# The local heads' v in alternate partitions: two requests a unit, keys in token order, a tile of its own

## The chip, the core and the metric

The kernel runs on one NeuronCore of one Trainium2 chip. The metric is the device time of one execution in microseconds (us). Five engines work beside each other: TensorE (PE; its weight loads are listed apart as PEld), VectorE (DVE), ScalarE (ACT), GpSimd (POOL) and SyncE (SP). SP issues all the DMA requests here. The profile is one execution with the hardware profiler on.

## What is computed

Three stages in float32, the output of each being the input of the next:

- Attention: B=4, 8 heads, S=576 tokens, D=64. Heads 0 to 3 are local (a query sees itself and the 31 tokens before it), heads 4 to 7 are strided (a query sees the earlier tokens with the same position modulo 32).
- A soft mixture of experts on the 2304 x 512 result: 8 experts with 4 slots each.
- A relu-squared layer, 512 to 2048 to 512.

```python
mask_local = (rel >= 0) & (rel < 32)              # rel = query position - key position
mask_strided = (rel >= 0) & (pos_k % 32 == pos_q % 32)
attn = softmax(where(mask, q @ k.T / 8, -1e9));  x = attn @ v
logits = x @ phi                                  # 2304 x 32
slot_in = softmax(logits, over tokens).T @ x      # 32 slots
slot_out = relu(slot_in @ w1[e]) @ w2[e]          # e: expert of the slot
y = softmax(logits, over slots) @ slot_out
out = relu(y @ w_in) ** 2 @ w_out
```

## The kernel before

**Units.** Attention is cut into 16 units of two heads of one batch. Units with an even number are local, those with an odd number strided. Each unit goes through short stages, and a table of token lists interleaves the stages of neighbouring units. The stages that matter here, for a local unit: `Tk`/`Tq` transpose k and q on PE (L504, L506), `k`/`q` copy them out of PSUM into `kTl` and `qTl` (64 features of head 0 on partitions 0 to 63, of head 1 on 64 to 127, all in the tile `space`); `S` computes scores (`st_S`, L557); `s` takes the maximum and adds it (`st_s`, L600); `e` exponentiates; `PT` transposes the weights into `Tl`; `p` copies; `A` multiplies by v (`st_A`, L677).

**Scores.** A local unit has 18 blocks of 32 queries. Each block sees 64 keys (its own 32 and the 32 before) of both heads, 128 columns in all: the moving operand of L566 is `kTl[:, :, 32qb:32qb+64]`, 64 columns of head 0 and then 64 of head 1. Each matmul runs as two instructions, so a unit has 36, in four streams (`tile_position`). The mask is added by matmuls in front (L562, L563). Within a block of 32 the keys lie with the 16 even tokens first and then the 16 odd ones.

**v of local units.** `vL` is a part of `space` with 128 partitions, 18 blocks and two heads of 65 columns (64 of v, and a column of ones that gives the softmax sum). Head h has partitions 64h to 64h+63: the upper 32 of them hold the block's own keys, the lower 32 the keys of the block before. `load_v` (L399) reads the block's own keys with four requests a unit: for each head one for the even and one for the odd tokens, each with 16 neighbouring partitions x 18 blocks x 256 bytes (72 KB). `shift_v` (L410) then copies on POOL, for each head, 32 partitions x 17 blocks x 64 columns from the upper 32 partitions to the lower, one block later. `vL` is single: the next local unit's load comes after the `A` of the one before.

**Order.** A scheduler sets SP's order of requests, the compute engines keep an order that is written out. Every SP request takes one of eight DMA lanes and waits for the request eight before it; where it overwrites a buffer it also waits for the engines that read it.

**Weights.** The experts' weights (w1 and w2, 64 requests of 512 KB) are fetched through SP into 27 ring slots and, as attention buffers retire, into the 16 slots of 4 KB a partition (`NA`) that make up `space` (`fetch`, L266, `give`, L299). After attention the first expert layer (L1055) frees slots for the last weights, the second (L1085) ends when they are there, and the last stage (L1241, L1283) follows on PE until the end.

Of the kernel before, what the change touches and what calls it, by code (L numbers as in the profile page):

```python
# [19 lines left out]
RING = 27  # L20
NA = 16
SPARE = 0
# [15 lines left out]
def kernel(  # L38
# [29 lines left out]

    space = wexp.enter_context(tc.tile_pool(name="space", bufs=1)).tile([128, NA * 1024], F32, name="space")
    at = [1024 * SPARE]  # L70
# [77 lines left out]
    def fill_last(n):  # L148
        if not n or spare[0] is None:
            return  # L150
        ps, c0 = spare[0]
        for _ in range(n):
            nc.tensor.matmul(
                out=ps[:, 1, c0:512], lhsT=identb,
                rhs=maskl.rearrange("p t h w -> p (t h w)")[:, 0:512 - c0], start=True, stop=True,
            )
# [109 lines left out]
    def fetch(n=RING):  # L266
        while stream and n:
            key = stream[-1]
            is_w = key[0] in ("w1", "w2")
            ring_ok = n_live[0] < (RING if is_w or key in so_[0:2] else late_cap[0])  # L270
            if is_w and free and not (ring_ok and given[0] == NA):
                r = free.pop(0)
                t = space[:, ts(r, 1024)]
# [40 lines left out]
    identb = cp.tile([128, 128], BF16, name="identb")  # L314
    identp = cp.tile([128, 128], BF16, name="identp")
    delta = cp.tile([128, 32], F32, name="delta")
# [5 lines left out]
    phi4 = cp.tile([128, KD, 4, NS], F32, name="phi4")  # L322
    none = cp.tile([128, 32], BF16, name="none")
    lN = cp.tile([128, B, 5, 32], F32, name="lN")
# [27 lines left out]
    ends["S", NU - 1] = at[0]  # L352
    vL, Pl, Tl = part(128, 18, 2, 65), part(128, 5, 2, 64), part(128, S)
    ends["A", NU - 2] = at[0]
# [4 lines left out]
    ends["X", NU - 1] = at[0]  # L359
    maskl = cp.tile([128, 5, 2, 64], BF16, name="maskl")  # L360
    assert at[0] <= NA * 1024, at[0]

# [27 lines left out]
    def load_v(u):  # L390
        if u >= NU:
            return
        b, p = units[u]
        for h in range(2):
            src = v[b, 2 * p + h]
            if local(u):
                for e in range(2):
                    r = 64 * h + 32 + 16 * e
                    nc.sync.dma_start(  # L399
                        out=vL[r:r + 16, :, h, 0:D], in_=src.rearrange("(b i e) d -> e i b d", i=16, e=2)[e]  # L400
                    )
            else:
                nc.sync.dma_start(
                    out=vS[64 * h:64 * h + 36], in_=src.rearrange("(p c) d -> p c d", c=16)
                )

    def shift_v(u):
        if local(u):
            for h in range(2):
                (nc.vector if on("vs", u)[h] else nc.gpsimd).tensor_copy(  # L410
                    vL[64 * h:64 * h + 32, 1:18, h, 0:D], vL[64 * h + 32:64 * h + 64, 0:17, h, 0:D]
                )

    def conv_in():
# [13 lines left out]
        done(key)  # L428

    load(0)  # L430
    load(1)
# [14 lines left out]
    for h in range(2):  # L446
        nc.vector.memset(kTl[ts(h, 64), h, 0:32], 0.0)
        nc.vector.memset(vL[64 * h:64 * h + 32, 0, h, 0:D], 0.0)
        nc.vector.memset(vL[ts(h, 64), :, h, D:D + 1], 1.0)
    nc.vector.memset(none, 0.0)  # L450
# [8 lines left out]
    for g in range(4):  # L459
        w_ = mf[ts(g, 32)].rearrange("p (b e i) -> p b e i", b=2, e=2)  # L460
        diag(w_, [[32, 2], [1, 2], [2, 16]], 0, NEG, op=ALU.is_gt, cm=-1)
        diag(w_, [[-32, 2], [-1, 2], [-2, 16]], 32, NEG, op=ALU.is_ge, cm=1)
    nc.vector.tensor_copy(
        maskl.rearrange("p t h w -> p (t h) w"), tmp[:, None, 0:64].to_broadcast([128, 10, 64])
    )
    nc.vector.memset(maskl[0:32, 0, :, 0:32], NEG)
    for g in range(4):
# [46 lines left out]

    def halves_(t, ps):

        for h in range(2):
            for e in range(2):
                o = t[ts(h, 64), h] if len(t.shape) == 3 else t[ts(h, 64)]
                i = ps[ts(e, 64), h].rearrange("c (j x) -> c j x", j=2)[:, :, 0:144]  # L520
                yield (
                    2 * h + e, o.rearrange("c (n e p j) -> c e n p j", e=2, p=8, j=2)[:, e],
                    i.rearrange("c j (n p) -> c n p j", p=8),
                )
# [32 lines left out]
    def st_S(u):  # L557
        ps = hold("s", u)
        if local(u):
            pf = flat(ps)[:, 0:640]  # L560
            mk = maskl.rearrange("p t h w -> p (t h w)")
# [33 lines left out]
    def st_s(u):  # L595
        ps = held.pop(("s", u))
        mx = ap_.tile([128, 16], F32, tag="mx", name="mx", bufs=3)
        if local(u):
            pv = flat(ps)[:, 0:640].rearrange("p (n w) -> p n w", w=64)
            nc.vector.tensor_reduce(out=mx[:, 0:10], in_=pv, axis=AX.X, op=ALU.max, negate=True)  # L600
            nc.vector.tensor_tensor(
                out=Pl.rearrange("p t h w -> p (t h) w"), in0=pv,
                in1=mx[:, 0:10, None].to_broadcast([128, 10, 64]), op=ALU.add,
            )
            return
# [14 lines left out]
    def st_e(u):  # L620
        P = Pl.rearrange("p t h w -> p (t h) w") if local(u) else Pe
        nc.scalar.activation(out=P, in_=P, func=AF.Exp)
# [13 lines left out]
    def st_PT(u):  # L636
        ps = hold("p", u)
        pf = flat(ps)
        if local(u):
            for t in range(5):  # L640
                nc.tensor.transpose(  # L641
                    out=pf[:, ts(t, 128)], in_=Pl[:, t].rearrange("p h w -> p (h w)"), identity=ident
                )
# [290 lines left out]
    def emit(u, token):  # L934
# [38 lines left out]
        elif what in ("S", "A"):  # L973
            give(what, v)

    for token in ("Tk+1", "k+1", "Tq+1", "q+1"):
# [358 lines left out]
```

## Time and profile before

| | |
|---|---|
| median of 3 runs | 407.06 us (402.96, 407.34, 407.06) |
| the profiled execution | 406.62 us, of which 404.9 us are the span from first to last instruction |
| mean granted TensorE clock | 0.975 of full speed |
| PE busy | 382.0 us, 94% of the span |
| DVE, ACT, POOL busy | 243.5, 235.0, 106.3 us |
| DMA | 69.88 MB, mean 173 GB/s |
| v of local units (L399) | 32 requests of 72 KB |
| chain that ended last, by line | L1283 47%, expert weights 10%, L1241 4%, v 4%, L677 2% |

A busy share is an average over the whole span. The attention stage ends near 140 us, the expert weights near 172 us, and from there to the end PE works almost without a gap, so the views of the first 175 us are read apart.

### The profile page before, as it was taken

The numbers are of one execution on the slowest core, as the hardware profiler recorded it, in microseconds if no ns is written. First come the engines' busy times: TensorE is split into PE (matmuls) and PEld (weight loads), VectorE is DVE, ScalarE is ACT, GpSimd is POOL, SyncE is SP. The second block draws the span as 40 slices with busy tenths as digits, with TensorE's granted clock in tenths as the row PEclk, the third lists the DMA queues.
The fourth block names the chain that finished last, engine by engine and source line by source line (L and its number), as shares of the span: only waits on it lengthen the run. The fifth ranks groups of instructions, "written<-read, shape, count | busy, mean of one in ns | idle before, by whom it ended". The sixth has DMA issues, their size and how long they took to land.

```text
span 404.9 us, 9258 instructions
## 1 busy us (share of the span) xinstructions
PE 382.0 (94%) x3649; PEld 301.0 (74%) x3649; DVE 243.5 (60%) x458; ACT 235.0 (58%) x491; POOL 106.3 (26%) x174
## 2 busy tenths in 40 slices
PE   7899999998947999999999999999999999999996
PEld 5688878877736635477787888888788888788885
DVE  5447588778743441158865666775768666755534
ACT  3457667766330320068777777667666766667670
POOL 6710221022002020035504544007522055320000
PEclk9689999999985999999999999999999999999999
DMA  7898899998999999997213203111000000003124
GB/s 159 256 281 200 258 268 236 284 250 237 402 319 357 355 345 418 418 418 284 104 53 105 88 31 132 64 53 53 2 0 2 1 0 2 0 26 131 63 94 155
DMA packets 38891, 69.88 MB, mean 173 GB/s; under 512 B 13312, under 2 KB 23808, under 8 KB 38848
## 3 DMA queue, kind: packets, MB, share of 16 engines
q1 hardware_dynamic: 38848, 69.29, 52.8%
q8 instruction: 29, 0.48, 0.5%
q14 instruction: 14, 0.11, 0.1%
HBM read 64.55 MB, written 4.72 MB: 171 GB/s over the span
## 4 chain that ended last, share of the span: by engine, by line
PE 68%; DMA 17%; DVE 5%; ACT 3%; POOL 2%; SPq 2%; issue 2%; DVEq 0%; POOLq 0%; ACTq 0%
PE banks L1283 47%; DMA w<-in_moe_w_dram 10%; DMA space<-in_v_dram 4%; PE banks L1241 4%; PE banks L677 2%; PE banks L504 2%; ACT space L492 2%; DMA space<-in_k_dram 2%; PE banks L506 2%; DVE space L662 1%; POOL space L410 1%; SPq L388 1%; PE banks L722 1%; PE banks L641 1%; DVE part L1297 1%
## 5 line engine op out<-in xcount | busy, mean ns | idle before, releaser
L1283 PE MATMUL banks<-w 128*128 128x512 f32 x867 | 217.0, 393 | 1.1 <-POOL w L1133 0.6
L1283 PEld LDWEIGHTS banks<-w 128*128 128x128 f32 x867 | 159.8, 188 | 36.6 <-DVE w L1257 1.5
L1257 DVE TENSOR_TENSOR w<-r,w 128x384 fp32r<-128x384 f32 (+1 forms) x97 | 59.3, 618 | 54.7 <-ACT w L1256 54.5
L1248 ACT ACTIVATE r<-banks 128x384 f32<-128x384 f32 (+1 forms) x96 | 47.0, 490 | 53.9 <-PE banks L1241 45.3
L492 ACT COPY space<-banks 64x288 f32<-64x288 f32 (+2 forms) x80 | 37.0, 463 | 32.8 <-DVE space L492 10.8
L1254 ACT ACTIVATE r<-r 128x384 f32<-128x384 f32 (+1 forms) x96 | 50.3, 524 | 3.0
L1256 ACT CAST w<-r 128x384 fp32r<-128x384 f32 (+1 forms) x97 | 49.5, 511 | 3.8 <-DVE r L1253 0.3
L410 POOL COPY space<-space 32x1088 f32<-32x1088 f32 x16 | 17.6, 1097 | 90.8 <-DMA space<-in_v_dram 66.4
L1297 DVE TENSOR_TENSOR part<-banks,part 128x512 f32<-128x512 f32 (+1 forms) x55 | 35.1, 675 | 1.9 <-PE banks L1283 1.9
L1241 PE MATMUL banks<-cT,A 128*128 128x384 f32 x96 | 32.0, 335 | 0.0
L220 POOL TENSOR_SCALAR nm<-w 128x512 f32<-128x512 f32 x28 | 21.6, 773 | 27.3 <-DVE w L227 14.7
L223 DVE TENSOR_SCALAR nm<-nm 128x512 uint32<-128x512 uint32 x32 | 14.7, 458 | 21.7 <-POOL nm L220 21.7
L1132 POOL CAST w<-wf 128x512 fp32r<-128x512 f32 x16 | 12.9, 809 | 50.5 <-PE banks L1283 27.1
L504 PE MATMUL banks<-ident,space 128*128 128x128 f32 x128 | 22.6, 304 | 1.3 <-DMA space<-in_q_dram 1.3
L1133 POOL TENSOR_TENSOR w<-wf,w 128x512 fp32r<-128x512 f32 x16 | 23.1, 1442 | 1.4
L224 DVE SCALAR_TENSOR_TENSOR nm<-w,nm 128x512 uint32<-128x512 uint32 x32 | 22.4, 700 | 1.1
L677 PE MATMUL banks<-space 128*32 128x130 f32 x288 | 14.5, 313 | 8.5 <-DMA space<-in_v_dram 5.8
L1241 PEld LDWEIGHTS banks<-cT,A 128*128 128x128 f32 x96 | 18.0, 188 | 3.8
L537 ACT ACTIVATE space<-banks 64x288 f32<-64x288 f32 (+1 forms) x35 | 15.9, 454 | 5.9 <-PE banks L506 3.9
L504 PEld LDWEIGHTS banks<-ident,space 128*128 128x128 f32 x128 | 16.1, 158 | 3.7 <-issue 1.7
L506 PEld LDWEIGHTS banks<-ident,space 128*128 128x128 f32 x128 | 18.8, 211 | 0.0
L677 PEld LDWEIGHTS banks<-space 128*32 128x32 f32 x288 | 10.4, 124 | 11.0 <-issue 6.2
(192 smaller groups left out, 443.1 us busy)
## 6 DMA issues: line engine op xcount, KB each, us to landing
w<-in_moe_w_dram SPq DMA_DIRECT2D x46, 512.0 KB
space<-in_moe_w_dram SPq DMA_DIRECT2D x18, 512.0 KB
w<-in_moe_w_in_dram SPq DMA_DIRECT2D x16, 512.0 KB
w<-in_moe_w_out_dram SPq DMA_DIRECT2D x16, 512.0 KB
out_dram<-part SPq DMA_DIRECT2D x17, 256.0 KB
space<-in_k_dram SPq DMA_DIRECT2D x16, 256.0 KB
space<-in_q_dram SPq DMA_DIRECT2D x16, 256.0 KB
space<-in_v_dram SPq DMA_DIRECT2D x32, 72.0 KB
```

The costliest lines, as they stand in the source:

```text
L492: return (nc.scalar.copy if act else nc.vector.tensor_copy)(out=out, in_=in_)
L504: nc.tensor.transpose(out=pf[:, 256 * t:256 * t + 128], in_=m[:, ts(t, 128)], identity=ident)
L506: nc.tensor.matmul(out=ps[:, h].rearrange("c (j x) -> c x j", j=2)[:, 128:144], lhsT=r, rhs=ident[:, ts(n, 64)].rearrange("k (p h) -> k h ...
L677: nc.tensor.matmul(out=pv[c, n // 4] if n < 18 else pv[c, 4].rearrange("p (h e) -> p h e", h=2), lhsT=w, rhs=i, start=True, stop=True, til ...
L1133: nc.gpsimd.tensor_tensor(out=lo, in0=r, in1=hi.bitcast(F32), op=ALU.subtract)
L1241: nc.tensor.matmul(out=ps[:, 0:HB], lhsT=A4[c][:, ts(f % QF, 128)], rhs=cT4[:, c0:c0 + HB], start=True, stop=True)
L1248: nc.scalar.activation(out=r[:, cuts[0]], in_=ps[:, cuts[0]], func=AF.Relu)
L1254: nc.scalar.activation(out=r[:, cuts[0]], in_=r[:, cuts[0]], func=AF.Square)
L1256: nc.scalar.copy(out=gh[:, x], in_=r[:, x])
L1257: nc.vector.tensor_tensor(out=gl[:, x], in0=r[:, x], in1=gh[:, x].bitcast(F32), op=ALU.subtract)
L1283: nc.tensor.matmul(out=acc[t][:, cs], lhsT=a[:, ts(t, 128)], rhs=wo[f][:, ts(w, 512)][:, cs], start=(first and k == 0), stop=(last and k = ...
L1297: nc.vector.tensor_tensor(out=pt[:, cs], in0=acc[t][:, cs], in1=pt[:, cs], op=ALU.add)
```

## The change

The tile `vL` leaves `space` and becomes a tile of its own, `vtile`, of 128 x 2340 floats. `space` keeps 14 slots; `vtile` gives two more for weights once `A` of unit 14 is done. Local v is loaded with two requests a unit, one for each head: the 32 tokens of a block go to partitions 64+h, 64+h+2, ... (144 KB each), so that the two heads alternate in the upper half. `shift_v` still has two copies, one for each head, now 64 partitions x 1088 elements from the upper half into the lower. The rows that hold the other head's tokens must meet zeros or masked weights, so keys of `S` alternate between heads too: `kTl` is in token order, the moving operand of L566 reads head 0 and head 1 by turns ("c h w -> c w h"), and the masks, `Pl` and the reduction of `st_s` follow. At the start one DVE memset clears the whole of `vL`, in place of several small ones on DVE and two on POOL, and DVE writes the ones. `identp` and `none` move into the last 80 columns of `space`.

```diff
-NA = 16
+NA = 14
+    vtile = sp.tile([128, 18 * 2 * 65], F32, name="vtile")
+    vL = vtile.rearrange("p (b h e) -> p b h e", b=18, h=2)
...
             if local(u):
-                for e in range(2):
-                    r = 64 * h + 32 + 16 * e
-                    nc.sync.dma_start(
-                        out=vL[r:r + 16, :, h, 0:D], in_=src.rearrange("(b i e) d -> e i b d", i=16, e=2)[e]
-                    )
+                nc.sync.dma_start(
+                    out=vL[64 + h:128:2, :, h, 0:D], in_=src.rearrange("(b r) d -> r b d", r=32)
+                )
...
-                    vL[64 * h:64 * h + 32, 1:18, h, 0:D], vL[64 * h + 32:64 * h + 64, 0:17, h, 0:D]
+                    vL[0:64, 1:18, h, 0:D], vL[64:128, 0:17, h, 0:D]
...
+    nc.vector.memset(vL, 0.0)
     load(0)
...
-        nc.vector.memset(vL[64 * h:64 * h + 32, 0, h, 0:D], 0.0)
-        nc.vector.memset(vL[ts(h, 64), :, h, D:D + 1], 1.0)
...
-    for h in range(2):
-        nc.gpsimd.memset(vL[ts(h, 64), :, 1 - h], 0.0)
...
+    nc.vector.tensor_copy(vL[:, :, :, D], sub2[:, None, :].to_broadcast([128, 18, 2]))
...
-            for n, o, x in halves_(kTl[:, :, 32:32 + S], ps):
+            for n, o, x in halves_(kTl[:, :, 32:32 + S], ps, "n p j e"):
...
-                    out=pf[ts(cg, 32), ts(t, 128)].rearrange("p (h w) -> p h w", h=2),
-                    lhsT=qTl[:, ts(qb, 32)], rhs=kTl[:, :, 32 * qb:32 * qb + 64],
+                    out=pf[ts(cg, 32), ts(t, 128)].rearrange("p (w h) -> p w h", h=2),
+                    lhsT=qTl[:, ts(qb, 32)], rhs=kTl[:, :, 32 * qb:32 * qb + 64].rearrange("c h w -> c w h"),
...
-            pv = flat(ps)[:, 0:640].rearrange("p (n w) -> p n w", w=64)
-            nc.vector.tensor_reduce(out=mx[:, 0:10], in_=pv, axis=AX.X, op=ALU.max, negate=True)
+            pv = flat(ps)[:, 0:640].rearrange("p (t w h) -> p t w h", t=5, h=2)
+            mt = mx[:, 0:10].rearrange("p (t h) -> p t h", h=2)
+            nc.vector.tensor_reduce(
+                out=mt, in_=pv.rearrange("p t w h -> p t h w"), axis=AX.X, op=ALU.max, negate=True
+            )
...
+            if (what, v) == ("A", NU - 2):
+                free.extend((NA, NA + 1))
```

The order of the compute engines is the same in both kernels but for the start. SP's order is not. The first place is SP around the last two v loads of local units (12 and 14; L399 before, L400 after are the local loads, L403 and L404 the strided ones, `w` and `space`/`vtile` from `in_moe_w_dram` the expert weights). Before:

```order
L399 DMA space<-in_v_dram 16x18x64 x4
L120 DMA w<-in_moe_w_dram 128x1024 x4
L120 DMA space<-in_moe_w_dram 128x1024
L120 DMA w<-in_moe_w_dram 128x1024 x4
L403 DMA space<-in_v_dram 36x1024 x2
L120 DMA w<-in_moe_w_dram 128x1024 x4
L120 DMA space<-in_moe_w_dram 128x1024
L399 DMA space<-in_v_dram 16x18x64 x4
L120 DMA space<-in_moe_w_dram 128x1024 x3
L403 DMA space<-in_v_dram 36x1024 x2
L120 DMA space<-in_moe_w_dram 128x1024 x11
```

With the change:

```order
L400 DMA vtile<-in_v_dram 32x18x64 x2
L123 DMA w<-in_moe_w_dram 128x1024 x5
L123 DMA space<-in_moe_w_dram 128x1024
L123 DMA w<-in_moe_w_dram 128x1024 x4
L404 DMA space<-in_v_dram 36x1024 x2
L123 DMA w<-in_moe_w_dram 128x1024 x3
L123 DMA space<-in_moe_w_dram 128x1024
L400 DMA vtile<-in_v_dram 32x18x64 x2
L123 DMA space<-in_moe_w_dram 128x1024 x3
L404 DMA space<-in_v_dram 36x1024 x2
L123 DMA space<-in_moe_w_dram 128x1024 x2
L123 DMA vtile<-in_moe_w_dram 128x1024 x2
L123 DMA space<-in_moe_w_dram 128x1024 x7
```

One weight request moved ahead of the strided load between them; the number of weight requests between the two local loads is 14 in both, and two v requests are gone from each group.

The second place is DVE at the start. Before:

```order
L173 MEMSET same 128x64
L443 MEMSET space 64x608
L444 MEMSET space 64x608
L447 MEMSET space 64x32
L448 MEMSET space 32x64
L449 MEMSET space 64x18
```

With the change:

```order
L176 MEMSET same 128x64
L431 MEMSET vtile 128x2340
L445 MEMSET space 64x608
L446 MEMSET space 64x608
L449 MEMSET space 64x32 x2
```

The memset of the whole of `vtile` comes ahead of the two that clear parts of `space`, and the small ones for `vL` are gone.

## Rows read from the trace of the kernel before

**Rows 1.** Stretches: start:end, length, busy time (instructions) by engine, PE clock, DMA share, GB/s
```profile
90.00:100.00 10.00, 9.59 (x188) 8.16 (x186) 8.13 (x13) 6.41 (x14) 1.28 (x2) 1.00 0.87 214
120.00:130.00 10.00, 6.38 (x54) 4.69 (x55) 2.43 (x5) 0.69 (x1) 2.19 (x2) 0.52 1.03 328
150.00:160.00 10.00, 10.00 (x156) 5.42 (x152) 1.38 (x2) 0.69 (x1) 0.00 (x0) 1.00 1.03 418
...
96.00:99.00 3.00, 2.90 (x81) 2.56 (x82) 2.65 (x5) 1.61 (x5) 0.34 (x1) 1.00 1.16 155
118.00:122.00 4.00, 0.00 (x0) 0.00 (x0) 1.14 (x4) 0.00 (x0) 0.06 (x1) 0.67 1.20 220
```

**Rows 2.** The chain of waits, 100 to 175 us: start, duration, what it waited for or ran
```profile
100.94 11.94 DMA w<-in_moe_w_dram
112.98 8.45 DMA space<-in_v_dram
...
121.94 1.09 POOL space L410
124.24 2.38 PE banks L677 x35
...
130.05 0.55 PE banks L719 x5
...
161.76 10.28 DMA w<-in_moe_w_dram
172.08 1.91 PE banks L1085 x26
```

**Rows 3.** PE's timeline: start, duration, instructions, and [idle before <-what ended it]
```profile
88.18 1.19 PE L677 MATMUL banks<-space 128*32 128x130 f32 x33 [0.68 <-POOL space L410]
91.66 1.18 PE L566 MATMUL banks<-space 128*32 128x128 f32 x34
...
116.16 0.82 PE L153 MATMUL banks<-maskl,identb 128*128 128x384 bf16 x4
122.82 0.61 PE L677 MATMUL banks<-space 128*32 128x130 f32 x2 [5.83 <-DMA space<-in_v_dram]
124.24 2.16 PE L677 MATMUL banks<-space 128*32 128x130 f32 x33 [0.81 <-POOL space L410]
...
190.19 2.21 PE L1283 MATMUL banks<-w 128*128 128x512 f32 x9
```

**Rows 4.** SP's timeline: requests in a row, start and the time to issue them
```profile
93.78 2.31 SPq L399 DMA_DIRECT2D space<-in_v_dram  x4
...
112.98 2.00 SPq L399 DMA_DIRECT2D space<-in_v_dram  x4
...
141.58 11.52 SPq L120 DMA_DIRECT2D w<-in_moe_w_dram  x14
```

**Rows 5.** Lines up to 175 us: busy us, mean ns | idle before, releaser
```profile
L410 POOL COPY space<-space 32x1088 f32<-32x1088 f32 x16 | 17.6, 1097 | 90.8 <-DMA space<-in_v_dram 66.4 <-PE banks L641 12.8 <-PE banks L586 11.2
L600 DVE TENSOR_REDUCE mx<-banks 128x10 f32<-128x640 f32 x8 | 6.6, 825 | 1.0 <-PE banks L572 0.8
L607 DVE TENSOR_REDUCE mx<-banks 128x16 f32<-128x288 f32 x8 | 3.7, 458 | 9.0 <-PE banks L586 9.0
L443 DVE MEMSET space<- 64x608 f32 x1 | 0.6, 565 | 0.1
L913 DVE TENSOR_REDUCE delta<-ident 128x32 f32<-128x128 f32 x1 | 0.4, 357 | 0.0
L917 DVE TENSOR_REDUCE gsel<-ident 128x4 f32<-128x128 f32 x1 | 0.3, 279 | 0.0
```

**Rows 6.** The score matmuls' weight loads: count, shortest/median/longest ns, first to last start
```profile
L566 PEld LDWEIGHTS banks<-space x288: 106/110/110, 9.6 to 107.6; 128*32 128x32 f32 x144
L586 PEld LDWEIGHTS banks<-space x512: 110/125/143, 15.5 to 116.0; 128*18 128x18 f32 x171
```

**Rows 7.** DVE's timeline at the start: start, duration, [idle before <-what ended it]
```profile
4.04 0.49 DVE L463 CAST maskl<-w 128x640 bf16<-128x640 f32 x1 [0.78 <-POOL w L437]
```

More of the change, by code (lines that the diff above doesn't have):

```diff
@@ L67 @@
     wexp = ExitStack()
-    space = wexp.enter_context(tc.tile_pool(name="space", bufs=1)).tile([128, NA * 1024], F32, name="space")
+    sp = wexp.enter_context(tc.tile_pool(name="space", bufs=1))
+    space = sp.tile([128, NA * 1024], F32, name="space")
+    vtile = sp.tile([128, 18 * 2 * 65], F32, name="vtile")
+    vL = vtile.rearrange("p (b h e) -> p b h e", b=18, h=2)
     at = [1024 * SPARE]
@@ L154, in fill_last @@
                 out=ps[:, 1, c0:512], lhsT=identb,
-                rhs=maskl.rearrange("p t h w -> p (t h w)")[:, 0:512 - c0], start=True, stop=True,
+                rhs=maskl.rearrange("p t w h -> p (t w h)")[:, 0:512 - c0], start=True, stop=True,
             )
@@ L272, in fetch @@
                 r = free.pop(0)
-                t = space[:, ts(r, 1024)]
+                t = space[:, ts(r, 1024)] if r < NA else vtile[:, ts(r - NA, 1024)]
             elif ring_ok:
@@ L314 @@
     identb = cp.tile([128, 128], BF16, name="identb")
-    identp = cp.tile([128, 128], BF16, name="identp")
+    identp = space[:, NA * 1024 - 64:NA * 1024].bitcast(BF16)
     delta = cp.tile([128, 32], F32, name="delta")
@@ L322 @@
     phi4 = cp.tile([128, KD, 4, NS], F32, name="phi4")
-    none = cp.tile([128, 32], BF16, name="none")
+    none = space[:, NA * 1024 - 80:NA * 1024 - 64].bitcast(BF16)
     lN = cp.tile([128, B, 5, 32], F32, name="lN")
@@ L352 @@
     ends["S", NU - 1] = at[0]
-    vL, Pl, Tl = part(128, 18, 2, 65), part(128, 5, 2, 64), part(128, S)
+    Pl, Tl = part(128, 5, 64, 2), part(128, S)
     ends["A", NU - 2] = at[0]
@@ L359 @@
     ends["X", NU - 1] = at[0]
-    maskl = cp.tile([128, 5, 2, 64], BF16, name="maskl")
-    assert at[0] <= NA * 1024, at[0]
+    maskl = cp.tile([128, 5, 64, 2], BF16, name="maskl")
+    assert at[0] <= NA * 1024 - 80, at[0]
     def local(u):
@@ L459 @@
     for g in range(4):
-        w_ = mf[ts(g, 32)].rearrange("p (b e i) -> p b e i", b=2, e=2)
-        diag(w_, [[32, 2], [1, 2], [2, 16]], 0, NEG, op=ALU.is_gt, cm=-1)
-        diag(w_, [[-32, 2], [-1, 2], [-2, 16]], 32, NEG, op=ALU.is_ge, cm=1)
+        diag(mf[ts(g, 32)], [[1, 64]], 0, NEG, op=ALU.is_gt, cm=-1)
+        diag(mf[ts(g, 32)], [[-1, 64]], 32, NEG, op=ALU.is_ge, cm=1)
     nc.vector.tensor_copy(
-        maskl.rearrange("p t h w -> p (t h) w"), tmp[:, None, 0:64].to_broadcast([128, 10, 64])
+        maskl, tmp[:, None, 0:64, None].to_broadcast([128, 5, 64, 2])
     )
-    nc.vector.memset(maskl[0:32, 0, :, 0:32], NEG)
+    nc.vector.memset(maskl[0:32, 0, 0:32, :], NEG)
     for g in range(4):
@@ L513, in blocks, with halves_ @@
         return flat(ps).rearrange("c (n x) -> c n x", n=4)[:, :, 0:144]
-    def halves_(t, ps):
+    def halves_(t, ps, order="n e p j"):
         for h in range(2):
@@ L521, in halves_ @@
                 yield (
-                    2 * h + e, o.rearrange("c (n e p j) -> c e n p j", e=2, p=8, j=2)[:, e],
+                    2 * h + e, o.rearrange("c (%s) -> c e n p j" % order, e=2, p=8, j=2)[:, e],
                     i.rearrange("c j (n p) -> c n p j", p=8),
@@ L560, in st_S @@
             pf = flat(ps)[:, 0:640]
-            mk = maskl.rearrange("p t h w -> p (t h w)")
+            mk = maskl.rearrange("p t w h -> p (t w h)")
             nc.tensor.matmul(out=pf[:, 0:512], lhsT=identp, rhs=mk[:, 0:512], start=True, stop=False)
@@ L598, in st_s @@
         if local(u):
-            pv = flat(ps)[:, 0:640].rearrange("p (n w) -> p n w", w=64)
-            nc.vector.tensor_reduce(out=mx[:, 0:10], in_=pv, axis=AX.X, op=ALU.max, negate=True)
+            pv = flat(ps)[:, 0:640].rearrange("p (t w h) -> p t w h", t=5, h=2)
[3 more added lines that the diff above has]
+            )
             nc.vector.tensor_tensor(
-                out=Pl.rearrange("p t h w -> p (t h) w"), in0=pv,
-                in1=mx[:, 0:10, None].to_broadcast([128, 10, 64]), op=ALU.add,
+                out=Pl, in0=pv, in1=mt[:, :, None, :].to_broadcast([128, 5, 64, 2]), op=ALU.add
             )
@@ L620, in st_e @@
     def st_e(u):
-        P = Pl.rearrange("p t h w -> p (t h) w") if local(u) else Pe
+        P = Pl.rearrange("p t w h -> p t (w h)") if local(u) else Pe
         nc.scalar.activation(out=P, in_=P, func=AF.Exp)
@@ L641, in st_PT @@
                 nc.tensor.transpose(
-                    out=pf[:, ts(t, 128)], in_=Pl[:, t].rearrange("p h w -> p (h w)"), identity=ident
+                    out=pf[:, ts(t, 128)], in_=Pl[:, t].rearrange("p w h -> p (w h)"), identity=ident
                 )
```

## The prediction

> **What bounds the kernel now.** I read the stretches of the span first. In 90 to 100 us PE is busy 9.59 of 10 us at full clock while the DMA engines move 214 GB/s [rows 1]: attention is bound by PE there. In 120 to 130 us PE is busy 6.38 us at a granted clock of 0.52, and DMA moves 328 GB/s at a share of 1.03; in 150 to 160 us DMA moves 418 GB/s. So from about 100 us on transfers set the pace, and 418 GB/s is what they reach undisturbed.
>
> The chain of waits says how [rows 2]. From 100.94 us it follows an expert weight for 11.94 us, which holds SP's next DMA lane, then v of unit 14 from 112.98 for 8.45 us, a shift copy at 121.94, and only at 124.24 the `A` of unit 14. From there PE runs attention out; the retiring buffers let SP issue the last 14 weights from 141.58 us [rows 4], the last one lands at 172.04 (161.76 + 10.28), and PE goes on at 172.08 [rows 2]. Those weights are issued behind the end of attention and need 30.5 us from there, so I let the end of the program move with `A` of unit 14, one to one. What the change does before 124 us counts in full where it is on this path; idle engines count nothing.
>
> PE's timeline gives the waits for v [rows 3]: 0.68 us at 88.18 for the shift copy of unit 10, 5.83 us and 0.81 us before `A` of unit 14. After that idle the same 33 matmuls take 2.16 us instead of 1.19: the clock had fallen to half. Until 130.05 the chain runs 5.8 us at this pace [rows 2]; at full clock it would be 5.8 x 1.19/2.16 = 3.2, so the low clock costs 2.6 us.
>
> **v's transfers.** While v of unit 12 flows, 96 to 99 us, 155 GB/s are moved in 3 us, 465 KB; at 418 GB/s they would take 1.1 us, so 1.9 us are lost. While v of unit 14 flows, 118 to 122 us, 220 GB/s in 4 us are 880 KB, worth 2.1 us, again 1.9 us lost [rows 1]. The DMA share stays above 1.1 in both: the engines are held, not idle. Each request goes to 16 neighbouring partitions; a new one has 32, with the same number of packets of the same 256 bytes. What slows them the trace doesn't show: if it is the packets, the gain is 0; if it is the narrow target, it is up to 1.9 us a load. I take twice the rate for v itself: a unit's 288 KB at some 140 GB/s (the 155 include other transfers) take 2.06 us, at 280 they take 1.03, so **1.0 us each for units 12 and 14**, between the bounds. Unit 10's v comes earlier too: its wait of 0.68 us before the copy and the like of 0.1 behind it go, **0.8 us**. Earlier units' v is waited for hardly at all.
>
> The trace shows 155 GB/s while the four requests of unit 12 are served [rows 1]. [...]
>
> Two v requests a unit less save SP about 2 x 0.5 us (four take 2.00 us at 112.98, 2.31 at 93.78 [rows 4]). SP waits for DMA lanes there, not for its own time, so I count 0; the bounds are 0 and 1.0 us.
>
> **The price in S.** The 36 score instructions of a unit now take head 0 and head 1 by turns, each column 608 floats away from the last. Now 34 of them take 1.18 us [rows 3]; with four streams 36 are 1152 columns a stream in 1.25 us, 1.08 ns a column. The last stage's matmuls, 9 of 512 columns in 2.21 us, pass a column in 0.48 ns, so S is not bound by reading alone, and a dearer read may be hidden in part. No row shows a moving operand with such a jump. The lower bound is 0. Nearest is DVE: a reduction of 128 elements that jumps takes 357 ns, one without 279 [rows 5], 0.61 ns an element more. Put on 1.08 this gives +0.7 us a unit; put on 0.48 it gives 1.09, nothing. The upper bound is from weight loads: 18 jumping columns take 125 ns, 32 plain ones 110 [rows 6], 6.9 against 3.4 ns a column, a factor of two, or +1.2 us a unit. I take **+0.4 us**, near the middle of the two readings of the DVE rows. Units 0 to 10 do six S before v of unit 12 is issued; in two of these DVE is late at that place anyway and hides about half, so **5 x 0.4 = 2.0 us** reach the path. S of units 12 and 14 fall into the 5.83 us of idle and cost nothing, unless that goes.
>
> [...]
>
> **What costs nothing.** The reduction at L600 now jumps by two in PSUM; with such jumps L607 takes 458 ns for 288 elements, 1.6 ns each, against 825 for 640, 1.3 [rows 5]. The difference may be its 16 outputs; the worst is 0.2 us a unit on DVE, which is on the chain once or twice: 0 to 0.4. The shift copies have twice the partitions and the same 1088 elements: 1097 ns as now [rows 5]. The DVE memset of 2340 elements takes some 2.2 us by L443's 565 for 608; DVE waits 0.78 us for POOL at 4.04 [rows 5, 7], and POOL is spared two memsets, so 0 to 1 us at the start. `vtile` gives its two slots at `A` of unit 14, not later than before. A weight moved ahead of the strided v between units 12 and 14 leaves the count between the local loads the same.
>
> **The sum.** -0.8 - 1.0 - 1.0 + 2.0 = -0.8 us. Against the profiled execution, 406.62, this is **405.8 us**. The median is 0.44 us above that execution, so against it the forecast is -0.3%, less than the 1% (403.0 to 411.1) that a measurement of this kernel tells from no change.
>
> **The rivals.**
>
> - *First: v moves as fast as its neighbours, and the clock holds.* Both lost 1.9 us come back, so the idle before unit 14 shrinks by 3.8 to 2.0 us, less S of units 12 and 14. PE was idle from 116.98 (116.16 + 0.82 [rows 3]), and the row of 118 to 122 with its mean of 0.67 shows the fall within it, about 2.5 us after the idle began. An idle of 2 us or less would then end before it, and 2.6 us come back. With S at +0.4: -0.8 - 3.8 - 2.6 + 2.0 = -5.2, **401.4**; with S free 399.4. For it: the share above 1.1 with little moved. Against it: the same packet size.
> [...]
> - *Third: the change does not do what it says to the transfers.* Packets stay 256 bytes and both requests lie in one half, so v drains as slowly as now. Then -0.8 + 2.0, or **407.8**.
> - *Fourth: S is free and v gains as forecast.* -2.8, **403.8**.
>
> **Chances and range.** The forecast 0.33, first 0.20, second 0.17, third 0.15, fourth 0.15. The first rival counts as faster, with a third of the fourth and a little of the forecast (SP's 1.0 saved): 0.27. Slower by over 1% are about half of the second, and what the third gives with a dear S (-0.8 + 5 x 1.06 = +4.5): 0.16. The rest, 0.57, is within 1%. The range from 400.5 to 411.5 leaves out the lower half of the first rival, the top of the second, and mishaps outside them all, together 0.2.
>
> **What would show it.** In the changed trace, the stretches in which v of units 12 and 14 flows: 250 to 300 GB/s by my forecast, over 400 by the first rival, about 150 by the third. [...] The wait before `A` of unit 10 is gone, and that of unit 14 is 3 to 4 us with the following rows at half clock. The last weights are issued 0.8 us earlier than 141.58, and the tail of 30.5 us stays. I am wrong if that tail changes, if a weight instead of v is what `A` of unit 14 waits for, or if DVE, not PE, paces S.

## The result

The changed kernel takes 408.06 us (median of 20 runs, 405.04 to 411.73), the kernel before, run beside it, 407.19 us (20 runs, 399.33 to 409.35). The means are 408.32 and 406.25, 2.1 us apart (by the spread of the runs 0.5 to 3.6). The ratio is 1.0132 with a 95% interval of 1.0088 to 1.0176. That ratio leaves out runs far above the fastest of their kernel, and as the kernel before spreads more, it keeps 6 of its 20 runs, so the means, 0.5% apart, are the better size. The same kernel run again (`again`, below) gives 1.0086 (1.0039 to 1.0134) and means 2.1 us apart; over both, 32 runs of the changed kernel have a mean of 408.44 us. It is **about 2 us slower**, where I had forecast 0.8 us less.

The profiled execution (406.44 us, span 404.7, clock 0.983) is one of the quicker ones. So its trace shows where the parts moved, and the means of all runs show what they are worth. One trace is one execution: `s_only` (below), whose v requests and order are those of before, waits 3.71 us for v of unit 14 where the kernel before waits 5.83. Differences of 1 or 2 us between two traces are therefore no measure of the change.

The stretches of the changed kernel, with the columns of [rows 1]; v of unit 12 flows in the fourth, v of unit 14 in the fifth:

```profile
90.00:100.00 10.00, 9.71 (x213) 8.31 (x206) 8.53 (x17) 6.25 (x14) 2.15 (x2) 1.00 0.89 272
120.00:130.00 10.00, 6.79 (x59) 5.06 (x61) 2.83 (x6) 0.69 (x1) 2.14 (x2) 0.66 1.03 319
150.00:160.00 10.00, 10.00 (x156) 5.48 (x152) 1.38 (x2) 0.69 (x1) 0.00 (x0) 1.00 1.03 412
93.00:96.00 3.00, 2.71 (x103) 2.24 (x101) 2.90 (x6) 1.84 (x4) 0.02 (x1) 1.00 1.14 236
115.00:121.00 6.00, 2.07 (x73) 1.22 (x71) 2.71 (x7) 2.04 (x5) 0.00 (x0) 1.00 1.18 212
```

Unit 12's v loses less than before: 236 GB/s in 3 us are 708 KB, worth 1.7 us at 418, so 1.3 us are lost where [rows 1] gave 1.9. Unit 14's loses more: 212 GB/s in 6 us are 1272 KB, worth 3.0 us, so 3.0 us are lost instead of 1.9. And the row of 150 to 160 us, in which nothing but weights flows, has 412 GB/s where it had 418: I had not expected the change to touch this place.

The chain of waits, as in [rows 2]:

```profile
98.99 11.91 DMA w<-in_moe_w_dram
...
110.98 10.46 DMA vtile<-in_v_dram
...
121.58 0.90 POOL vtile L411
122.62 1.11 POOL vtile L411
123.78 2.38 PE banks L677 x35
...
161.20 10.54 DMA w<-in_moe_w_dram
171.79 1.91 PE banks L1087 x26
```

PE's timeline, as in [rows 3]:

```profile
97.90 1.47 PE L677 MATMUL banks<-vtile,space 128*32 128x130 f32 x35
104.24 1.42 PE L564 MATMUL banks<-space 128*32 128x128 f32 x34
113.33 1.22 PE L686 MATMUL banks<-space 128*64 128x72 f32 x32 [3.62 <-DMA space<-in_v_dram]
122.58 0.61 PE L677 MATMUL banks<-vtile,space 128*32 128x130 f32 x2 [5.51 <-DMA vtile<-in_v_dram]
123.78 2.16 PE L677 MATMUL banks<-vtile,space 128*32 128x130 f32 x33 [0.59 <-POOL vtile L411]
```

Two rows of the kernel before stand against the first and the third of them, `A` of unit 12 and the strided unit 13:

```profile
100.97 1.18 PE L677 MATMUL banks<-space 128*32 128x130 f32 x33 [0.79 <-POOL space L410]
113.23 1.22 PE L686 MATMUL banks<-space 128*64 128x72 f32 x32 [1.28 <-DMA space<-in_v_dram]
```

SP's timeline of the changed kernel:

```profile
91.55 1.32 SPq L400 DMA_DIRECT2D vtile<-in_v_dram  x2
...
110.98 2.06 SPq L400 DMA_DIRECT2D vtile<-in_v_dram  x2
...
140.94 11.64 SPq L123 DMA_DIRECT2D w<-in_moe_w_dram  x14
```

These rows show a lead that is lost. v of units 12 and 14 is issued 2.2 and 2.0 us earlier than in [rows 4]. But v of unit 14 needs 10.46 us instead of 8.45, and lands when it did. PE's lead has become waiting: 3.62 us before the strided unit 13, where it was 1.28, and 5.51 before unit 14, where it was 5.83 and after which the clock is at half as before. `A` of unit 14 comes 0.46 us earlier, the last weights are issued 0.64 us earlier, and the tail takes 30.85 us (140.94 to 171.79) instead of 30.5.

The single lines, as in [rows 5] and [rows 6]:

```profile
L411 POOL COPY vtile<-vtile 64x1088 f32<-64x1088 f32 x16 | 17.2, 1104 | 89.4 <-DMA vtile<-in_v_dram 72.2 <-PE banks L641 9.2 <-PE banks L156 8.0
L599 DVE TENSOR_REDUCE mx<-banks 128x10 f32<-128x640 f32 x8 | 6.6, 824 | 3.6 <-PE banks L570 3.4 <-PE banks L564 0.2
L431 DVE MEMSET vtile<- 128x2340 f32 x1 | 2.0, 2008 | 0.4 <-issue 0.4
```

```profile
L564 PEld LDWEIGHTS banks<-space x288: 106/110/173, 9.9 to 105.4; 128*32 128x32 f32 x144
L564 PE MATMUL banks<-space x288: 299/301/423, 9.9 to 105.5; 128*32 128x128 f32 x144
```

The score matmul before:

```profile
L566 PE MATMUL banks<-space x288: 272/273/298, 9.6 to 107.7; 128*32 128x128 f32 x144
```

Copy, reduction (824 ns against 825) and memset are as costed. The median score matmul takes 301 ns instead of 273.

### The profile page after: what moved, and what is told of

It is laid out like the page before. It is cut to its first block, busy times and chain, and to the rows that moved or that the text cites. A ratio compares the mean times of both kernels' runs of the same rounds, so it can differ in the third digit from the quotient of the medians.

```text
span 404.7 us, 9235 instructions
## 1 busy us (share of the span) xinstructions
PE 380.9 (94%) x3649; PEld 299.5 (74%) x3649; DVE 243.3 (60%) x456; ACT 235.6 (58%) x491; POOL 103.7 (26%) x172
## 4 chain that ended last, share of the span: by engine, by line
PE 72%; DMA 16%; SPq 4%; DVE 3%; POOL 2%; ACT 1%; issue 1%; DVEq 0%; POOLq 0%; ACTq 0%
PE banks L1285 47%; DMA w<-in_moe_w_dram 7%; DMA vtile<-in_v_dram 4%; DMA space<-in_k_dram 4%; PE banks L1243 4%; PE banks L1057 3%; PE banks L1087 2%; PE banks L502 2%; SPq L391 2%; PE banks L564 2%; PE banks L677 2%; PE banks L504 1%; SPq L123 1%; POOL vtile L411 1%; DVE part L1299 1%
## 5 line engine op out<-in xcount | busy, mean ns | idle before, releaser
L411 POOL COPY vtile<-vtile 64x1088 f32<-64x1088 f32 x16 | 17.2, 1104 | 89.4 <-DMA vtile<-in_v_dram 72.2
L502 PE MATMUL banks<-ident,space 128*128 128x128 f32 x128 | 21.4, 292 | 1.7 <-DMA space<-in_q_dram 1.7
L677 PE MATMUL banks<-vtile,space 128*32 128x130 f32 x288 | 12.9, 295 | 6.6 <-DMA vtile<-in_v_dram 5.5
L502 PEld LDWEIGHTS banks<-ident,space 128*128 128x128 f32 x128 | 15.3, 152 | 4.3 <-DMA space<-in_q_dram 1.8
L504 PE MATMUL banks<-ident,space 128*128 128x32 f32 x128 | 17.8, 263 | 0.0
L504 PEld LDWEIGHTS banks<-ident,space 128*128 128x128 f32 x128 | 17.8, 201 | 0.0
```

Of the source, the lines that this page charges most:

```text
L502: nc.tensor.transpose(out=pf[:, 256 * t:256 * t + 128], in_=m[:, ts(t, 128)], identity=ident)
L504: nc.tensor.matmul(out=ps[:, h].rearrange("c (j x) -> c x j", j=2)[:, 128:144], lhsT=r, rhs=ident[:, ts(n, 64)].rearrange("k (p h) -> k h ...
```

## The experiments

My theories changed with each group of runs, and they are told in that order. "Mean" is over all runs of a kernel; beside it stands the mean of the kernel before, run beside that group. The ratios are of the kind above.

**The parts.** In `s_only` only the score operand reads by turns.

```diff
-                    out=...rearrange("p (h w) -> p h w", h=2), rhs=kTl[:, :, 32 * qb:32 * qb + 64],
+                    out=...rearrange("p (w h) -> p w h", h=2),
+                    rhs=kTl[:, :, 32 * qb:32 * qb + 64].rearrange("c h w -> c w h"),
```

> Kernel before with one edit: the moving operand and the output of the score matmuls read head 0 and head 1 by turns, v, masks and requests as before (weights then meet other rows of v, so the result is not the reference's). SP's order is that of before. Theory A (the by-turns operand is what costs): the score matmul goes from a median of 273 ns to 301 ns, as in the changed kernel, 9 x 28 ns = 0.25 us a unit; five units' worth, 1.3 us, reach the issue of v of unit 12, and the time is 0.5 to 1.5 us above before. Theory B (v's transfers cost, since both new requests lie in the upper half of the partitions): S may show 301 ns, but the end does not move by more than 0.4 us, since transfers set the pace from 100 us on. Theory C (the two kernels are the same within the spread of runs): no difference beyond the interval.

Mean 406.71 (12 runs) against 406.03 (29), ratio 1.0002 (0.9962 to 1.0041). The price is there in the matmuls, and in the time no difference can be told; `s_only`'s own row:

```profile
L566 PE MATMUL banks<-space x288: 299/301/423, 11.0 to 109.2; 128*32 128x128 f32 x144
```

`v_only` is the changed kernel with this edit undone.

> Changed kernel with the score matmuls' moving operand and output back to head 0 first, then head 1 (273 ns expected); v's two requests, own tile, masks and reduction as in the change (weights then meet other rows of v, so the result is not the reference's). SP's order is that of the change. Theory A: the time falls by 0.5 to 1.5 us against the changed kernel and is at or below before. Theory B: v of unit 14 flows at about 150 to 200 GB/s for 5 us as in the changed kernel, and the time stays 1 to 2 us above before. Theory C: the same as before within the interval.

Mean 408.07 (12 runs), ratio 1.0043 (1.0001 to 1.0085), 2.0 us above before on the mean, as theory B has it. The score operand is not what makes the change slow. `halves` and `runs32` ask whether the half of the partitions is:

```diff
+  # halves: kernel before, keys in token order, two requests
+                out=vL[64 * h + 32:64 * h + 64, :, h, 0:D], in_=src.rearrange("(b r) d -> r b d", r=32)
+  # runs32: changed kernel, neighbouring partitions, S operand plain, Pl written in two pieces
+                out=vL[64 + 32 * h:96 + 32 * h, :, h, 0:D]
```

> Kernel before with two requests a unit: head 0's own keys in partitions 32 to 63 and head 1's in 96 to 127, 32 neighbouring partitions each, keys in token order, score operand plain; no tile of its own, shift copies as before; the result is the reference's. Only the half of the partitions differs from runs32 in what the requests do. Theory B: here the two requests lie in both halves, so v of unit 14 flows 1 us shorter than in the changed kernel (above 250 GB/s in the stretch), and the time is 1 to 2 us below runs32 and v_only and at or below before. Theory A: as v_only, within 0.5 us. A rival, packets: 256-byte packets set the rate, whatever the partitions, and v flows at 150 to 220 GB/s in all of them.

> Changed kernel with head 0's own keys in partitions 64 to 95 and head 1's in 96 to 127 instead of by turns; the score operand is plain, and the addition of the maximum is two instructions that write the weights in that order; own tile and shift copies as in the change; the result is the reference's. Theory A: time as v_only, 0.5 to 1.5 us below the changed kernel. Theory B: v of unit 14 as slow as in the changed kernel, time 1 to 2 us above halves. Packets rival: the same as halves.

`halves`: mean 407.95 (12 runs), ratio 1.0014 (0.9971 to 1.0057), so not clearly slower than before nor faster. `runs32`: mean 411.18 (6 runs), ratio 1.0106 (1.0048 to 1.0164); its column of ones still goes by turns, so its softmax sums are not the reference's. As the expectation of theory B has it, `runs32` is slower than `halves` (by 3.2 us), but its addition in two pieces and its tile of its own differ too, so this pair settles nothing on the half of the partitions.

**SP's order.** The scheduler gives both kernels different orders of requests. `after_order_before` and `before_order_after` swap them, by a chain of order dependencies over all requests but the output's.

```diff
+    prev = None
+    for c in SP_ORDER:              # the other kernel's order, one name for each request
+        ins = spq[c[0]][int(c[1:])]
+        if prev is not None:
+            behind(ins, prev)
+        prev = ins
```

> The changed kernel itself once more, beside the kernel before on one chip. Theory B' (the two larger v requests and the order of SP's requests that comes with them cost; the score operand costs little): mean of all runs 1.5 to 2.5 us above before, as in the first comparison (408.32 against 406.25, 20 runs each). Theory C (only spread of the start): the means agree within 0.8 us.

> Changed kernel with SP's requests held in the order that they have in the kernel before (two v requests stand where four stood); the result is the reference's. Theory D (the moved order costs: a weight more goes ahead of the strided v of unit 13, and units 3 to 6 are fetched in another sequence): the time falls to 0.5 us or less above before, and the wait for v of unit 13 is back at about 1.3 us instead of 3.6. Theory E (the form of the requests costs, whatever the order): it stays 1.5 to 2.5 us above before, and v of unit 14 takes 10 us from issue to landing against 8.5.

> Kernel before (four v requests of 16 partitions) with SP's requests in the order that they have in the changed kernel; the result is the reference's. Theory D: 1 to 2 us slower than before, wait for v of unit 13 about 3.6 us. Theory E: same as before within 0.5 us, v of unit 14 lands 8.5 us after its issue.

`again`: mean 408.66 (12 runs) against 406.57 (23), ratio 1.0086 (1.0039 to 1.0134): the slowness is real. `after_order_before`: mean 411.16 (6 runs), 1.0125 (1.0069 to 1.0180), 4.6 us above before and above what either theory had. `before_order_after`: 405.38 (12 runs), 0.9994 (0.9958 to 1.0031). The moved order costs the kernel before nothing, though it does bring back a long wait for the strided unit 13 (here of `before_order_after`, PE's timeline):

```profile
114.67 2.19 PE L706 MATMUL banks<-space 128*64 128x72 f32 x32 [3.76 <-DMA space<-in_v_dram]
122.78 0.38 PE L697 MATMUL banks<-space 128*32 128x130 f32 x2 [2.20 <-DMA space<-in_v_dram]
```

So a weight that moves ahead of v of unit 13 makes PE wait there (3.76 us against 1.28), and less before unit 14 (2.20 against 5.83): the same transfers, another place. With the order ruled out, I looked for the cause in the form of the requests.

**The transfers by themselves.** `micro` is a kernel of its own, with `load_v`'s request written in four forms:

```diff
+            o = {
+                "turns": t[64 + h:128:2, :, h, 0:D],
+                "halves": t[64 * h + 32:64 * h + 64, :, h, 0:D],
+                "upper": t[64 + 32 * h:96 + 32 * h, :, h, 0:D],
+            }[kind]                 # "quarter": the four requests of before
```

> A kernel that only moves data and computes nothing of the reference: four phases, each with v of four local units (1.15 MB in 256-byte packets) and nothing beside it, in the forms of before (16 neighbouring partitions a request), of the change (32 alternate partitions of the upper half), in both halves (32 to 63 and 96 to 127), and 32 neighbouring ones in the upper half; then eight weights of 512 KB alone, and eight weights with three units of v among them in each of the four forms. If the narrow target sets the rate: the change's form is 1.6 to 2 times as fast as the one of before. [...] If the 256-byte packets set it: all four agree within 15%, near 200 GB/s (18 ns a packet on each of 16 engines). Among weights the same order holds; weights alone 410 to 420 GB/s.

Stretches of `micro` while v flows alone, beside memsets on DVE (columns: start:end, length, DVE, POOL, clock, DMA share, GB/s): before's form, the change's and both halves with four units each; the fourth is the neighbouring 32 of the upper half, three units.

```profile
18.00:21.00 3.00, 3.00 (x1) 0.00 (x0) 1.00 1.47 107
38.50:45.00 6.50, 5.02 (x4) 0.00 (x0) 1.00 1.29 165
57.50:63.50 6.00, 4.81 (x1) 0.00 (x0) 1.00 1.30 187
...
187.50:192.50 5.00, 0.00 (x0) 0.00 (x0) 1.00 1.31 173
```

Alone, 16 neighbouring partitions a request are worst, 107 GB/s, the change's form gives 165 and both halves 187. The packets theory, under which all agree within 15%, falls. Both halves are 1.13 times as fast as the change's form. The narrow target's 1.6 to 2 is nearly met (1.54). The scheduler issued all the weights ahead of v, so nothing is told of v among weights.

In the kernels the gain is partly lost. The 9216 packets of 256 bytes in each trace give what a unit's v takes of the 16 engines' time. Four narrow requests: 2.33 us in the kernel before, 2.24 in `tile_alone` (below), 2.06 to 2.11 in `s_only`, `token_keys` and `before_order_after`. Two requests by turns: 2.20 to 2.29 in SP's order of the change (the changed kernel, `again`, `v_only`), 2.05 to 2.10 in that of before (`after_order_before`, `order_before_2`, `v_only_ob`). Four requests by turns: 1.97 (`four_requests`, below). Two requests of 32 neighbouring partitions: 2.13 in the upper half (`runs32`), 1.74 to 1.88 in both halves, in six traces. So **the by-turns form in the upper half drains among weights no faster than four narrow requests, and the same two requests in both halves do.** The difference is 0.2 to 0.5 us a unit; no run shows what in the half makes it.

**Each part in one order.** All in SP's order of before. `two_requests` is the kernel before with two requests in both halves and nothing else; `token_keys` has its keys, mask and rows in token order, still with four requests; `four_requests` is the changed kernel with each request cut in two.

```diff
+  # two_requests
+                out=vL[64 * h + 32:64 * h + 64, :, h, 0:D], in_=src.rearrange("(b r) d -> r b d", r=32)
+  # token_keys
-                        ... in_=src.rearrange("(b i e) d -> e i b d", i=16, e=2)[e]
+                        ... in_=src.rearrange("(b e i) d -> e i b d", i=16, e=2)[e]
+            for n, o, x in halves_(kTl[:, :, 32:32 + S], ps, "n p j e"):
+  # four_requests
+                for lo in (0, 16):
+                        out=vL[64 + h + 2 * lo:64 + h + 2 * lo + 31:2, :, h, 0:D],
+                        in_=src.rearrange("(b r) d -> r b d", r=32)[lo:lo + 16],
```

> Kernel before with one edit: two v requests a unit of 32 neighbouring partitions (token order; the rows no longer match the keys' order, so the result is not the reference's), SP's requests held in the order of before. Theory N (the number of requests costs: the two missing ones leave SP two lanes ahead, so more weights stand in front of v, q and k): mean of all runs 1.5 to 2 us above before. Theory K (token order of the keys costs): same as before within 0.6 us.

> Kernel before with keys, mask and v rows in token order and still four v requests of 16 partitions, SP's requests held in the order of before; the result is the reference's. ACT's k copies write every second element (406 ns instead of 392 on the mean of 57). Theory K: 1 to 2 us above before, since ACT's four k copies of a unit lie in front of S. Theory N: same as before within 0.6 us.

> Changed kernel with four v requests a unit of 16 alternate partitions each, SP's requests held in the order of before; the result is the reference's. Theory N: the mean falls to 0.5 to 1 us above before (what is left is the score operand's 273 to 301 ns). Theory K: 1.5 to 2.5 us above before, as the changed kernel.

> The changed kernel in SP's order of before once more, as the partner of four_requests on one chip: 2 to 4 us above before on the mean by both theories; the difference to four_requests is the number of requests alone, 1.5 us or more by theory N, under 0.6 us by theory K.

`two_requests`: mean 405.61 (12 runs) against 406.54 (28, one of 608.27 us left out), ratio 0.9953 (0.9919 to 0.9987). `token_keys`: 406.79 (12), 1.0003 (0.9970 to 1.0036). `four_requests`: 412.07 (6), 1.0128 (1.0078 to 1.0178). `order_before_2`: 409.33 (12), 1.0087 (1.0053 to 1.0121). Theories N and K both fall: fewer requests cost nothing, in the changed kernel too (409.33 against 412.07), and token order costs nothing that can be told. `four_requests`, 5.5 us above before, lies above what either theory had. `order_before_2` is the very kernel of `after_order_before`: 2.8 us above before here, 4.6 there, so such differences are known to some 2 us. What was left was the tile.

The trace of `two_requests` shows what I had described as the first rival, in this one execution: an idle of 1.86 us instead of 5.83, and the matmuls behind it at full clock, in 1.19 us. Its span is 399.5 us.

```profile
119.25 0.38 PE L694 MATMUL banks<-space 128*32 128x130 f32 x2 [1.86 <-DMA space<-in_v_dram]
120.70 1.19 PE L694 MATMUL banks<-space 128*32 128x130 f32 x33 [1.06 <-POOL space L427]
```

In `two_requests_2` (below) the idle is 3.88 us and the clock is at half after it, so this is had in some executions only.

```profile
123.11 0.61 PE L694 MATMUL banks<-space 128*32 128x130 f32 x2 [3.88 <-DMA space<-in_v_dram]
124.53 2.16 PE L694 MATMUL banks<-space 128*32 128x130 f32 x33 [0.81 <-POOL space L427]
```

**The tile.** `own_tile` adds the tile alone to `two_requests`, `tile_alone` adds it to the kernel before.

```diff
-NA = 16
+NA = 14
...
+    vtile = sp.tile([128, 18 * 2 * 65], F32, name="vtile")
...
+    identp = space[:, NA * 1024 - 64:NA * 1024].bitcast(BF16)
...
+    none = space[:, NA * 1024 - 80:NA * 1024 - 64].bitcast(BF16)
...
+            if (what, v) == ("A", NU - 2):
+                free.extend((NA, NA + 1))
```

> two_requests with v in a tile of its own, 14 slots and two behind A of unit 14, identp and none at the end of space; nothing else (v's rows do not match the keys' order, so the result is not the reference's); SP's order of before. Theory T (the tile costs): 2 us or more above two_requests, so 407.5 or more. Theory sum (small prices of S and token order add up): as two_requests, 404.5 to 406.5.

> The changed kernel in SP's order of before with the score operand head by head (weights meet other rows of v, so the result is not the reference's). Theory S (27 ns more a matmul are paid in full by PE while it is the bound, 0.25 us a unit and 1.3 to 2 us in all): 1.3 to 2 us below order_before_2 (mean 409.3), so about 407.5. Theory T: within 0.6 us of order_before_2.

> two_requests with the keys and the mask in token order, so that the result is the reference's; v in space, head 0 in partitions 32 to 63 and head 1 in 96 to 127; score operand head by head; SP's order of before. If token order costs nothing: 405 to 406 and 0.3 to 0.6% below before, the version to keep. If its longer ACT copies count (0.1 us a unit): 406 to 407.

> Kernel before with one edit: v in a tile of its own with 14 + 2 slots (identp and none at the end of space); four requests, keys, rows and score operand as before, SP's order of before; the result is the reference's. Theory T: 1.5 to 3 us above before (mean near 408 to 409). Theory chance (the earlier difference was spread): within 0.8 us of before.

> own_tile once more (two requests and the own tile). Theory T: 2 to 3 us above two_requests_2. Theory chance: within 0.8 us of it.

> two_requests once more. Two requests alone: 0.3 to 0.8% below before again, mean 404.5 to 406. If the first result was chance: as before.

| kernel | tile of its own | mean, runs | before, runs | ratio and interval |
|---|---|---|---|---|
| `tile_alone` | yes | 410.19, 6 | 406.41, 23 | 1.0111 (1.0053 to 1.0169) |
| `own_tile` | yes | 409.03, 6 | 405.83, 17 | 1.0110 (1.0060 to 1.0160) |
| `own_tile_2` | yes | 409.45, 12 | 406.41, 23 | 1.0070 (1.0023 to 1.0117) |
| `two_requests_2` | no | 405.97, 12 | 406.41, 23 | 0.9983 (0.9942 to 1.0024) |
| `halves_ob` | no | 406.58, 12 | 405.83, 17 | 1.0001 (0.9964 to 1.0039) |
| `v_only_ob` | yes | 411.31, 6 | 405.83, 17 | 1.0166 (1.0115 to 1.0218) |

**The tile of its own, with what comes with it, costs the time**: alone on the kernel before it costs 3.8 us (2.4 to 5.2 by the spread of the runs), on `two_requests_2` 3.5 (1.3 to 5.6). Both pairs are in SP's order of before; no run takes the tile alone out of the changed kernel in its own order. `v_only_ob`, 5.5 us above before, lies above both of its theories. `halves_ob`, the version to keep if token order had been free and two requests a gain, does not beat the kernel before. Only `two_requests` once did beyond its interval; its second interval reaches to no change, and its rows do not match its keys.

The tile leaves its mark in the stretch 150 to 170 us, in which only weights flow, nearly all of them into ring slots; `two_requests_2` and then `tile_alone` (columns as in [rows 1]):

```profile
150.00:170.00 20.00, 20.00 (x285) 10.33 (x281) 2.07 (x3) 1.37 (x2) 0.85 (x2) 1.00 1.03 418
```

```profile
150.00:170.00 20.00, 20.00 (x259) 9.50 (x252) 2.82 (x4) 2.53 (x4) 2.23 (x4) 1.00 1.02 409
```

This row reads 418 to 420 GB/s in seven traces with v in `space` (before, `s_only`, `before_order_after`, both `two_requests`, `token_keys`, `halves_ob`) and 408 to 411 in ten with the tile (the changed kernel, `again`, `v_only`, `four_requests`, `v_only_ob`, both in the order of before, both `own_tile`, `tile_alone`). `halves` and `runs32` end attention some 6 us later, and other traffic falls into that stretch. A 4096-byte packet in it takes 159.5 ns on the mean in the kernel before, nearly all within 158 to 159; in the changed kernel 162.5, and more than half of them 160 to 169.

Most of the time is lost ahead of that stretch, as SP's issue of the last 14 weights shows; `two_requests_2` and then `tile_alone`:

```profile
141.69 10.83 SPq L136 DMA_DIRECT2D w<-in_moe_w_dram  x14
```

```profile
145.24 11.72 SPq L140 DMA_DIRECT2D w<-in_moe_w_dram  x14
```

From this issue to the end of the span the ten traces with the tile need 0.6 us more on the mean than the seven without (264.0 against 263.4). In SP's order of before the issue itself comes at 143.7 us on the mean in the seven traces with the tile and at 139.7 in the six without. At the issue of v of unit 4 the tile's traces are 1.2 us behind, at that of unit 12 2.7: the price builds up through attention.

What the tile changes for all buffers is their place. To fit, `identp` (256 bytes a partition) and `none` (64) left the pool of constants, which lies in front of the ring, and so ring and `space` start 320 bytes lower: at byte 24768 and 145600 of a partition instead of 25088 and 145920.

Two more sets of packets go with the place. The output, written from 363 us on, leaves in 2176 packets of 2048 bytes from a tile that moved by the same 320 bytes: 99% of them take at most 84 ns in each of the eight traces with v in `space` (mean 84), 27 to 29% in each of the eleven with the tile (mean 87). And `micro`, which has neither ring nor slots nor attention and whose weights and zeros start at byte 53952 and 103104, shows the same: 31% of its 2048-byte packets, which write the zeros out, take at most 84 ns. Of its eight weights on their own (from 70 us on), 23% and 53% of the packets of the sixth and the seventh take 160 to 169 ns, and at most 2% of the first five. Not every packet to or from these tiles is long: in the changed kernel the long ones are under a tenth from 148 to 153 us and seven tenths from 158 us on. What else it takes stays open.

That the place of a tile is what makes its packets 3 ns longer is my estimate from these three sets of packets. No run moves `micro`'s tiles, and none puts the base back with the tile kept, so **the 320 bytes are the likely reason, not a shown one**; against the slots as the reason stands `micro`, which has none.

The size fits in part. A trace has 12864 packets of 4096 bytes; 3 ns more of each on 16 engines are 2.4 us, of which those of the saturated 72 us from 100 us on (some 6500 packets, 27 MB) count in full, 1.2 us. Measured were 2.1 us for the changed kernel and 3.5 to 3.8 for the tile in SP's order of before. The 1024-byte packets of q and k, which flow during attention, are longer as well: 57.8 to 62.2 ns on the mean in the ten traces, 55.3 to 58.8 in the seven. All packets together take 4.9 us more of the 16 engines' time in `tile_alone` than in the kernel before, and 6.1 more in `own_tile_2` than in `two_requests_2`. How much of this PE waits for was not followed, so the remainder stays open.

## Why the prediction was wrong

- **The tile cost nothing in my working**, and only the two slots were considered. This is the step that failed. The tile alone costs the kernel before 3.8 us (`tile_alone`, 410.19 against 406.41), enough to turn -0.8 into a loss. I read in the diff that `identp` and `none` move, and took it for a matter of room. They move every address behind them, and with the move go longer packets (162.5 against 159.5 ns for 4096 bytes).
- **What bounds it** held: transfers from 100 us on, the end of attention as the gate, a tail of 30.5 us (30.85 here). The 0.35 us more are no measure, since the tails of traces without the tile differ by more.
- **v's transfers, -1.0 us each** failed too. The row of unit 12 loses 0.6 us less, that of unit 14 loses 1.1 more, and a unit's v needs nearly as much engine time as before (2.26 against 2.33 us). I had halved the transfer because the target doubles. `micro` shows that gain alone (165 against 107 GB/s) and the kernel does not show it among weights; the third rival, with both requests in one half, pointed the right way: in both halves they took 1.74 to 1.88 us.
- **-0.8 us at unit 10** came at most in part: that wait is gone, and the bulk of `A` of unit 12 started 3.1 us ahead (97.90 against 100.97). But v of unit 10 was already issued 2.0 us ahead (76.5 against 78.5), so some 1.1 us are left for it, in one trace of each. They were lost again to v of units 13 and 14. I should have asked what is late next, not only what is early.
- **The price in S**, +0.4 us a unit, was too high: 28 ns for each of nine steps of four streams are 0.25 us, and in the time no difference can be told (`s_only`). A factor of two in S, which the second rival's chance stands for, is shown by no run: the score matmul rose by a tenth (301 against 273 ns). The DVE rows that I took it from were a poor measure: the reduction of 357 ns also writes 32 results where the one of 279 writes 4, and the reduction of `st_s` takes 824 ns with jumps and 825 without.
- **The clock in the first rival** was read from a single fall, and two other traces show how little that tells: behind PE's idle of 3.62 us before unit 13 the changed kernel's 32 matmuls ran at full clock (granted 1.00, 1.22 us), behind 3.76 us in `before_order_after` at half (granted 0.50, 2.19 us).
- The third rival, 407.8, comes nearest in time. Its mechanism, v as slow as before, did occur, but its 2.0 us for S were not felt, and the tile was in none of the rivals: its nearness is luck. The measured 408.06 lies in the range, which is luck as well; the direction was wrong.

## What to carry to other kernels

When an edit adds or removes a tile, look where it moves the tiles behind it, and compare the rate of a stretch that only moves data: 418 against 409 GB/s showed here what no engine's row did. But a stretch that shows a mark need not be where the time goes: compare when each stage starts, over several traces. Fewer, wider requests drained faster here where they lay in both halves (1.7 to 1.9 us of engine time a unit against 2.0 to 2.3), though the time did not show it clearly. And a wait that an edit removes ahead of a saturated stretch may only move: look for the next transfer that PE will reach too early (here v of the strided unit 13: 3.62 us of waiting where it was 1.28).

## What was not expected of the hardware

Tiles that start 320 bytes lower go along with 2% longer 4096-byte packets into them (162.5 against 159.5 ns in the changed kernel and the one before; 408 to 411 against 418 to 420 GB/s in ten traces and seven) and 4% longer 2048-byte packets out of them (87 against 84 ns in eleven traces and eight). Alone (`micro`), 256-byte packets into 16 neighbouring partitions move at 107 GB/s and into 32 of them in each half at 187, in packets of the same size. A moving operand that jumps 608 floats with each element costs a tenth (301 against 273 ns).
